# A list of further products of zeros, in other tilings of TensorE's array, behind the first 22: an attention and gMLP block on one core

## The chip, the core and the metric

The kernel runs on one NeuronCore of one Trainium2 chip. The metric is the time of one execution on the device, in microseconds (us). The engines are PE (TensorE, the matrix engine; its weight loads are shown as PEld), DVE (VectorE), ACT (ScalarE), POOL (GpSimd) and SP (SyncE, which issues most DMAs). Each works through its own queue in order, and they wait for each other by semaphores.

## The reference

One token sequence x of 2048 rows and 512 columns is normalised, and the sum of x, an attention block and a gated MLP of the normalised x is returned. All data are float32.

```python
# S, D, H = 2048, 512, 32;  Dh = 16;  F = 1792, Fh = 896
def _A_ref(x, wqkv, wo):
    q, k, v = split(x @ wqkv)                    # 32 heads of 16
    p = softmax(q @ k.T * Dh ** -0.5)
    return (p @ v) @ wo
def _B_ref(x, w_in, w_sp, b_sp, w_out):
    z = gelu(x @ w_in)
    z1, z2 = z[..., :Fh], layernorm(z[..., Fh:])
    g = w_sp @ z2 + b_sp[:, None]                # over the 2048 rows
    return (z1 * g) @ w_out
xn = layernorm(x)
return x + _A_ref(xn, wqkv, wo) + _B_ref(xn, w_in, w_sp, b_sp, w_out)
```

## The kernel before

The instructions of every engine are written out in an order that the program fixes while it is built (a manual schedule). A planner inside it keeps a clock of its own for each engine and decides from these clocks which product comes next; on the chip only the resulting order and the semaphores count.

**Opening.** The four groups of 512 rows of x are loaded (`load_x`), together with the weights of the first query and key columns and of the values. Then come, on PE, `WARM` = 22 products of zeros: `zeror` (128 x 128 zeros, stationary) times `brow` (128 x 512 zeros, streamed) into one bank of the PSUM tile `dps`. They use the type float32r, which PE takes in one pass; plain float32 is taken in two. Behind them a list of words, `STEPS`, is worked off by the class `First`, one method for each letter. The words that matter here, with their rows and columns as digits:

- S, R, N: statistics of two blocks of 128 rows on DVE (`s`), the scale by ACT's square root and DVE's reciprocal (`r`, L1044 to L1046), the normalisation by POOL (`n`, L1055).
- T: four transposes of 128 x 128 on PE into a PSUM tile (`t`, L1060). E: the block is split into a high part by ACT and a rest by DVE (`e`, through `split`, L244).
- Q: twelve products of 128 rows and 512 columns for a query or key block (`q`, through `mm3`, L247 to L249). F: their result is split and stored to scratch memory. L: loaded back as stacks.
- VH, VL, V, VE: weights and products of the values. M, X: the first products for the maxima of the scores (L1132) and their reduction on DVE (L1137).

The four PSUM tiles `dps`, `sl[0]`, `sl[1]`, `sl[2]` (two banks each) are taken in turn by T, Q, V and M, beginning with `sl[0]`. The order of the words begins like this; each engine gets its part in this order:

```python
STEPS = (
    "S00 S01 R00 WH0 N00 WL0 R01 N01 S10 S11 T01 T02 WH1 R10 E01 R11 T00 N11 T03 E02 WL1 N10 E00 VH2* E03 S21 ..."
```

**Steady part.** After the opening, PE works in turns. A turn has score blocks (L1245, two products on row halves that run side by side), blocks for the maxima (L1259, likewise), slots of dense work (L1310: projections, MLP and spatial products, each slot a pair on the two row halves), and then the values (`values`, L1352): 16 products of plain float32, each with 128 rows and 32 columns of the array, four column quarters side by side. Where PE would have nothing to do, a pair of zeros is put in (`filler`, L1324). ACT takes the exponentials, DVE the maxima (L840), POOL splits weights. At the end come the last normalisations and output products, among them products on groups of 32 rows (L984). A matmul's tiling of the array follows from its operands: the partitions on which they start, the number of rows, and the number of columns.

Of the kernel before, what the change touches and what calls it, by code (L numbers as in the profile page):

```python
# [16 lines left out]
P = 128  # L17
# [30 lines left out]
WARM = 22  # L48
# [20 lines left out]
def fused_block(ctx, tc, x, wqkv, wo, w_in, w_spT, b_sp, w_out, out):  # L69
    nc = tc.nc  # L70
# [28 lines left out]
    zeror = cp.tile([P, P], F32R, name="zeror")  # L99
# [3 lines left out]
    brow = cp.tile([P, 512], F32R, name="brow")  # L103
# [29 lines left out]
    dps = ps.tile([P, 2, 512], F32, tag="d", name="dps", bufs=1)  # L133
    sl = [ps.tile([P, 2, 512], F32, tag=f"s{i}", name=f"sl{i}", bufs=1) for i in range(3)]
# [3 lines left out]
    def raw(t):  # L138
        return t.bitcast(F32) if t.dtype == F32R else t
# [999 lines left out]
    def init_rows(a, put):  # L1139
        for j in range(2):  # L1140
            row = 64 * j + KS
            for r in range(2):
                put(kst[a][row + r:row + r + 1, :], cscr[0:1, :])

    engines = {mybir.EngineType.PE, mybir.EngineType.Activation, mybir.EngineType.DVE, mybir.EngineType.Pool, mybir.EngineType.SP}
    with tc.manual_schedule(engines=engines):
# [15 lines left out]
        braw = t512("braw")[0:16, 0:P]  # L1162
        move(braw, b_sp)
        init_rows(0, move)
        for _ in range(WARM):
            nc.tensor.matmul(dps[:, 1, :], zeror, brow, start=True, stop=True)
        first = First(w0r, w0, wvr, wv, braw)
        for word in STEPS.split():
            first.step(word)
# [302 lines left out]
```

## Time and profile before

| | |
|---|---|
| time, median of 2 runs | 1834.91 us (1834.79 and 1835.03) |
| span of the profiled execution, first to last instruction | 1830.4 us (its own time is not listed apart from the two runs) |
| PE busy | 1800.6 us, 98% of the span, 14742 matmul records |
| DVE, ACT, POOL busy | 1443.2, 1211.4, 684.5 us |
| products of zeros at the start | 2.01 to 9.72 us |
| granted TensorE clock, mean | 0.999 |

The profile shows one execution. Each view gives rows with a start and a duration, both in us, the engine, the line of the kernel (L1166 is line 1166), the operation, the tiles (output<-inputs), the shapes and a count. For a matmul, "64*128 64x512" is the part of the array that its weights take (rows times columns) and the streamed operand. Matmuls are pipelined and their ends are modelled, so that a row's duration contains time in which the next matmul runs already; from start to start is the safer measure. A wait ends with what released it, shown behind "<-".

### The profile page before, as it was taken

The page shows a single profiled execution, that of the slowest core. Times are in us where ns is not written, and L with a number is a line of the kernel's source. Part 1 is how long each engine was busy: PE and PEld are TensorE (multiplying, and loading weights), DVE is VectorE, ACT ScalarE, POOL GpSimd, SP SyncE. Part 2 cuts the span into 40 slices and gives each one's busy share as a digit, 9 for nine tenths or more (in the row PEclk, how much of TensorE's full clock was granted, in tenths as well). Part 3 has the DMA queues.
Part 4 walks back from the last instruction along what each step waited for, and adds up shares of the span by engine and source line. Part 5 has one row for each costly group of instructions (what it writes and reads, how often), then busy time and mean ns, then how long its engine had stood idle before and what let it go on. Part 6 is the DMA issues. An engine that isn't in the chain of part 4 may idle for free.

```text
span 1830.4 us, 38100 instructions
## 1 busy us (share of the span) xinstructions
PE 1800.6 (98%) x14742; PEld 1087.6 (59%) x14742; DVE 1443.2 (79%) x1696; ACT 1211.4 (66%) x1329; POOL 684.5 (37%) x786
## 2 busy tenths in 40 slices
PE   9999999999999999999999999999999999999998
PEld 6666566666556565565656655656566665656543
DVE  8857787888888787787877887778778877888882
ACT  4257777888877777666666665666666665666655
POOL 5452241777767776212532244103422140002201
PEclk9999999999999999999999999999999999999999
DMA  7876654433664237647757568655757477466423
GB/s 265 280 240 227 201 190 128 123 114 114 180 190 132 95 105 209 163 137 186 227 144 204 159 188 201 166 143 158 190 146 181 141 210 170 121 156 168 136 88 104
DMA packets 214910, 305.64 MB, mean 167 GB/s; under 512 B 37744, under 2 KB 107952, under 8 KB 214720
## 3 DMA queue, kind: packets, MB, share of 16 engines
q1 hardware_dynamic: 207240, 275.93, 53.3%
q0 software_dynamic: 7488, 27.27, 4.3%
q8 instruction: 116, 1.90, 0.4%
q14 instruction: 66, 0.54, 0.1%
HBM read 193.27 MB, written 109.85 MB: 166 GB/s over the span
## 4 chain that ended last, share of the span: by engine, by line
PE 89%; DVE 5%; DMA 3%; issue 1%; SPq 1%; ACT 1%; POOL 0%; DVEq 0%; ACTq 0%; POOLq 0%
PE dps L1310 35%; PE sl L1352 24%; PE sl L1245 14%; PE sl L1259 12%; DVE mm L840 4%; PE dps L1324 1%; SPq L142 1%; DMA wsp_14r<-in_w_spT 1%; DMA zs<-z2scr 1%; DMA mscr<-ms 0%; PE sl L984 0%; DMA x<-in_x 0%; ACT pf L86 0%; DMA qst<-mscr 0%; DMA qst<-qscr 0%
## 5 line engine op out<-in xcount | busy, mean ns | idle before, releaser
L840 DVE TENSOR_REDUCE mm<-sl 128x2 f32<-128x1024 f32 x1008 | 1208.3, 1222 | 186.0 <-PE sl L1259 177.4
L86 ACT ACTIVATE pf<-sl 128x1024 f32<-128x1024 f32 x1024 | 1043.1, 1026 | 326.7 <-PE sl L1245 288.6
L1352 PE MATMUL sl<-pf,vall 128*32 128x512 f32 x4096 | 467.9, 595 | 0.6 <-DVE on L974 0.6
L1245 PE MATMUL sl<-qst,kst 50*128 50x512 f32 x2048 | 434.6, 417 | 7.7 <-DVE mm L840 2.2
L1259 PE MATMUL sl<-kst,qst 48*128 48x512 f32 x2016 | 414.9, 404 | 3.9 <-DVE mm L840 2.6
L1310 PE MATMUL dps<-wsp,zs 64*128 64x512 f32 x2352 | 381.6, 392 | 0.9 <-DMA zs<-z2scr 0.6
L1245 PEld LDWEIGHTS sl<-qst,kst 50*128 50x128 f32 x2048 | 194.4, 184 | 220.3 <-issue 81.6
L1352 PEld LDWEIGHTS sl<-pf,vall 128*32 128x32 f32 x4096 | 119.2, 109 | 266.5 <-issue 234.9
L1259 PEld LDWEIGHTS sl<-kst,qst 48*128 48x128 f32 x2016 | 191.8, 185 | 104.2 <-ACT pf L86 49.5
L1310 PEld LDWEIGHTS dps<-wsp,zs 64*128 64x128 f32 x2352 | 228.7, 187 | 36.8 <-DMA zs<-z2scr 1.2
L86 ACT ACTIVATE e<-sl 128x512 f32<-128x512 f32 x64 | 38.3, 598 | 189.9 <-PE sl L1352 177.8
L1374 DVE TENSOR_TENSOR e<-sl,e 128x512 f32<-128x512 f32 x64 | 44.2, 691 | 130.2 <-PE sl L1352 80.5
L743 POOL TENSOR_TENSOR hhl<-z1i,hhl 128x512 fp32r<-128x512 f32 x28 | 35.9, 1292 | 280.6 <-ACT hhl L86 280.6
L1310 PE MATMUL dps<-w,xt 64*128 64x448 f32 x768 | 110.5, 368 | 1.7
L1310 PE MATMUL dps<-wout,hp 64*128 64x512 f32 x672 | 110.5, 393 | 0.1
L891 POOL TENSOR_TENSOR ob<-ob 128x512 f32<-128x512 f32 (+1 forms) x16 | 20.6, 1287 | 173.0 <-DMA ob<-rscr 173.0
L1310 PEld LDWEIGHTS dps<-w,xt 64*128 64x128 f32 x768 | 73.7, 186 | 16.1 <-issue 8.4
L1310 PEld LDWEIGHTS dps<-wout,hp 64*128 64x128 f32 x672 | 64.2, 187 | 10.4 <-issue 0.6
L397 POOL TENSOR_TENSOR qkhl<-qr,qkhl 128x512 fp32r<-128x512 f32 x24 | 30.3, 1280 | 97.3 <-ACT qkhl L86 83.0
L887 POOL TENSOR_TENSOR ob<-ob 128x512 f32<-128x512 f32 (+1 forms) x16 | 20.6, 1287 | 99.3 <-DMA ob<-escr 99.3
L1310 PE MATMUL dps<-wf,zs 64*128 64x512 f32 x336 | 55.5, 392 | 0.1
L1310 PE MATMUL dps<-xnT,wqk 64*128 64x512 f32 x288 | 47.9, 394 | 0.3
(298 smaller groups left out, 1692.4 us busy)
## 6 DMA issues: line engine op xcount, KB each, us to landing
zs<-z2scr SPq DMA_DIRECT2D x192, 256.0 KB
escr<-e SPq DMA_DIRECT2D x60, 256.0 KB
hscr<-hhl POOLq DMA_DIRECT2D x28, 512.0 KB, 5.9
qst<-qscr SPq DMA_DIRECT2D x60, 192.0 KB
kst<-kscr SPq DMA_DIRECT2D x60, 192.0 KB
qscr<-qkhl SPq DMA_DIRECT2D x16, 512.0 KB
kscr<-qkhl SPq DMA_DIRECT2D x16, 512.0 KB
xt<-xscr SPq DMA_DIRECT2D x64, 128.0 KB
```

What stands on the lines that cost most here:

```text
L86: return nc.scalar.activation(out, in_, func, **kw)
L142: nc.sync.dma_start(raw(dst), raw(src))
L397: nc.gpsimd.tensor_sub(hl[:, 1, :], raw_, hl[:, 0, :].bitcast(F32))
L743: nc.gpsimd.tensor_sub(hl[:, 1, :], z1, hl[:, 0, :].bitcast(F32))
L840: nc.vector.tensor_reduce(mmax[g][:, :, t, kc], sl[k], AX.X, ALU.max)
L887: nc.gpsimd.tensor_add(both_[rows, 0, :], both_[rows, 0, :], both_[rows, 1, :])
L891: nc.gpsimd.tensor_mul(both_[rows, 0, :], both_[rows, 0, :], both_[rows, 1, :])
L1245: nc.tensor.matmul(sl[k][:, j, :], kst[p % 2][rows, kt * P:(kt + 1) * P], qst[p % 2][rows, c * 512:(c + 1) * 512], start=True, stop=True)
L1259: nc.tensor.matmul(sl[k][:, j, :], qst[p % 2][rows, tt * P:(tt + 1) * P], kst[p % 2][rows, kc * 512:(kc + 1) * 512], start=True, stop=True)
L1310: nc.tensor.matmul(bank_of(bank)[:, :w], lhs, rhs, start=go, stop=stop)
L1352: nc.tensor.matmul(sl[k][cols:cols + VW, 0, :], vpack(kt + r, 2 * p + j), pf[:, j * 512:(j + 1) * 512], start=n % CYC == 0, stop=n % CYC = ...
L1374: nc.vector.tensor_add(e, sl[k][:, 0, :], e)
```

## The change

Behind the 22 products stands a list of 112 more, before the first word of `STEPS`. All of them multiply zeros by zeros; nothing reads the results. `halves_of` issues pairs on the two row halves into the two banks of `dps`, with 512 or 16 streamed columns and 128, 64 or 32 columns of the array; `whole` issues products on all 128 rows, with 128, 64 or 32 columns; `quarters` issues four plain float32 products on the four column quarters into one bank of `sl[0]`; `eighths` issues eight, on the four quarters and two row halves, into both banks of `sl[0]`.

```diff
-        for _ in range(WARM):
-            nc.tensor.matmul(dps[:, 1, :], zeror, brow, start=True, stop=True)
+        def halves_of(n, cols=512, m=P):
+            for _ in range(n):
+                for b, r in enumerate((0, 64)):
+                    nc.tensor.matmul(dps[:m, b, :cols], zeror[r:r + 64, :m], brow[r:r + 64, :cols], start=True, stop=True)
+
+        def whole(n, m=P):
+            for _ in range(n):
+                nc.tensor.matmul(dps[:m, 1, :], zeror[:, :m], brow, start=True, stop=True)
+
+        def quarters(n):
+            for _ in range(n):
+                for u in range(4):
+                    cols = slice(32 * u, 32 * u + 32)
+                    nc.tensor.matmul(sl[0][cols, 0, :], raw(zeror)[:, cols], raw(brow), start=True, stop=True)
+
+        def eighths(n):
+            for _ in range(n):
+                for u in range(4):
+                    cols = slice(32 * u, 32 * u + 32)
+                    for b, r in enumerate((0, 64)):
+                        nc.tensor.matmul(sl[0][cols, b, :], raw(zeror)[r:r + 64, cols], raw(brow)[r:r + 64], start=True, stop=True)
+
+        whole(WARM)
+        for fn, *a in ((halves_of, 3), (quarters, 2), (halves_of, 3), (eighths, 2), (halves_of, 3), (halves_of, 1, 16), (quarters, 2), (halves_of, 1, 16), (halves_of, 3),
+                       (quarters, 2), (whole, 3), (quarters, 2), (whole, 3), (halves_of, 3), (halves_of, 4, 512, 64), (whole, 4, 64), (whole, 4, 32), (halves_of, 4, 512, 32)):
+            fn(*a)
         first = First(w0r, w0, wvr, wv, braw)
         for word in STEPS.split():
             first.step(word)
```

## The prediction

> **What bounds the kernel now.** I read the page's first part and its chain first, then the order of instructions at the start, since the edit stands there.
>
> ```profile
> span 1830.4 us, 38100 instructions
> PE 1800.6 (98%) x14742; PEld 1087.6 (59%) x14742; DVE 1443.2 (79%) x1696; ACT 1211.4 (66%) x1329; POOL 684.5 (37%) x786
> PE 89%; DVE 5%; DMA 3%; issue 1%; SPq 1%; ACT 1%; POOL 0%; DVEq 0%; ACTq 0%; POOLq 0%
> ```
>
> PE is busy for 98% of the span and carries 89% of the chain that ended last. Whatever makes the start of the real work later is therefore unlikely to be made good afterwards: there is 30 us of PE idle in the whole span (1830.4 - 1800.6). Next, the order of instructions at the start. Columns: start, duration, engine, line, operation, tiles, shapes, count, and in brackets the idle time before and what ended it.
>
> ```profile
> 2.01 7.87 PE L1166 MATMUL dps<-brow,zeror 128*128 128x512 f32 x22 [2.01 <-POOL brow L104]
> 9.72 0.27 PE L1060 MATMUL sl<-ident,x 128*128 128x128 f32 x1
> 11.73 1.20 PE L1060 MATMUL sl<-ident,x 128*128 128x128 f32 x9 [0.42 <-POOL x L1055]
> 12.09 0.60 ACT L86 ACTIVATE xnT<-sl 128x512 fp32r<-128x512 f32 x1 [0.51 <-PE sl L1060]
> 13.01 0.68 DVE L244 TENSOR_TENSOR xnT<-sl,xnT 128x512 fp32r<-128x512 f32 x1
> 13.61 0.15 DVE L1045 RECIPROCAL rs<-rs 128x2 f32<-128x2 f32 x1
> 14.06 3.45 POOL L1055 TENSOR_SCALAR x<-x,rs 128x512 f32<-128x512 f32 x4 [2.38 <-DVE rs L1046]
> 17.57 0.98 PE L1060 MATMUL sl<-ident,x 128*128 128x128 f32 x7 [0.23 <-POOL x L1055]
> ```
>
> The 22 products of zeros hold PE from 2.01 to 9.72; then the first transposes of x come, and the fourth of them (11.73) waits for POOL. So about 2 us of what is put between the zeros and the transposes would be hidden by work that PE waits for anyway. Behind that stands a loop through the engines: ACT splits the transposed block (step E01, 12.09), DVE takes the rest (13.01), then DVE finishes the second pair's scale (13.61), then POOL normalises four rows (14.06), then PE transposes them (17.57). ACT and DVE are in order, and the second pair's square root and reciprocal stand behind E01. So if E01 is late, POOL's 14.06 and PE's 17.57 are late by as much.
>
> The opening by stages: busy time of PE, PEld, DVE, ACT, POOL, each with its count, then granted clock and DMA; below it, what PE waits for from 13 to 55 us.
>
> ```profile
> 9.50:13.00 3.50, 2.42 (x17) 1.68 (x16) 3.27 (x10) 1.01 (x3) 2.17 (x3) 1.00 1.04 384
> 13.00:18.00 5.00, 4.22 (x21) 2.80 (x20) 4.90 (x12) 2.34 (x6) 3.94 (x5) 1.00 1.04 381
> 18.00:33.00 15.00, 15.00 (x84) 12.33 (x82) 14.01 (x34) 10.93 (x23) 11.49 (x13) 1.00 0.54 190
> 33.00:55.00 22.00, 22.00 (x106) 15.85 (x105) 18.05 (x20) 5.58 (x10) 2.02 (x3) 1.00 0.72 249
> 55.00:60.00 5.00, 4.23 (x19) 2.71 (x18) 3.35 (x4) 0.60 (x1) 0.00 (x0) 1.00 0.96 374
> 60.00:80.00 20.00, 17.59 (x136) 12.35 (x134) 16.25 (x19) 6.01 (x7) 14.95 (x20) 1.00 0.90 285
> PE sl L247 <- DVE xnT L244: 0.4, 1, 0.4
> PE sl L1060 <- POOL x L1055: 0.2, 1, 0.2
> PE sl L249 <- DVE xnT L244: 0.2, 1, 0.2
> ```
>
> From 13 to 18 DVE is busy for 4.90 of 5; from 18 to 55 PE is busy without a gap; from 13 to 55 PE's waits are 0.8 us in all. So there is no slack behind E01 that a delay could eat: first DVE sets the pace, then PE.
>
> **What the change adds.** Nothing is removed, no wait is added, and no DMA moves. Behind the 22 products stand 112 products of zeros, all on PE and in front of the first transpose. They write dps and sl[0], which PE itself overwrites later, in its own order. I need the price of each tiling.
>
> ```profile
> 14.55 0.39 PE L247 MATMUL sl<-xnT,wqk 128*128 128x512 f32 x1
> 15.47 0.39 PE L248 MATMUL sl<-xnT,wqk 128*128 128x512 f32 x1
> 107.73 1.54 PE L1310 MATMUL sl<-kst,xnT 64*128 64x512 f32 x12
> 109.09 1.54 PE L1310 MATMUL dps<-qst,xnT 64*128 64x512 f32 x12
> 24.94 0.44 PE dps L1060 x4
> 31.80 0.39 PE L249 MATMUL sl<-xnT,wqk 128*128 128x512 f32 x1
> 32.12 0.50 PE L1132 MATMUL sl<-kst,qst 48*128 48x512 f32 x2
> 32.55 0.66 PE L1060 MATMUL sl<-ident,x 128*128 128x128 f32 x4
> 33.04 0.60 PE L1060 MATMUL dps<-ident,x 128*128 128x128 f32 x4
> 87.61 0.41 PE L1310 MATMUL dps<-kst,xnT 64*128 64x512 f32 x2
> 87.95 3.64 PE L1352 MATMUL sl<-pf,vall 128*32 128x512 f32 x32
> 91.52 0.50 PE L1245 MATMUL sl<-qst,kst 50*128 50x512 f32 x2
> 91.86 0.40 PE L1259 MATMUL sl<-kst,qst 48*128 48x512 f32 x2
> 115.02 3.64 PE L1352 MATMUL sl<-pf,vall 128*32 128x512 f32 x32
> 118.59 0.50 PE L1245 MATMUL sl<-qst,kst 50*128 50x512 f32 x2
> 1814.52 1.13 PE L984 MATMUL sl<-sel,on 32*128 32x512 f32 x4
> 1815.58 1.07 PE L1352 MATMUL sl<-pf,vall 128*32 128x512 f32 x8
> ```
>
> The short row at 24.94 is one of the chain's pieces: start, time that it holds on the chain, engine, tile, line, count. Durations of matmuls overlap, so I go by starts.
> - Whole rows, 512 columns: L247 at 14.55 and L248 at 15.47 are four products apart, (15.47 - 14.55) / 4 = 0.23 us each.
> - A row pair: twelve records are six pairs, (109.09 - 107.73) / 6 = 0.227; 0.23 taken. Two halves together cost what one whole product costs.
> - A switch of tiling, there and back: from 31.80 to 33.04 run a whole product (0.23), a pair (0.23) and four transposes (0.44 by the row at 24.94), 0.90 in all. It took 1.24, so 0.34 for two switches, 0.17 each.
> - Column quarters on plain float32: one turn of the attention values is 16 products in the code and 32 records in the trace, so a float32 product is two records. From 87.61 to 91.86 stand two pairs (0.46), two switches (0.34) and four sets of four quarters: (4.25 - 0.80) / 4 = 0.86 a set.
> - Eighths (half the rows, a quarter of the columns, float32): not in the trace. The nearest row is L984, two float32 products on different row groups and banks: 1815.58 - 1814.52 = 1.06, switches included. One after the other they would be two times 0.86, so row groups run side by side. I take a set of eight at 0.86; the other end is 1.72, if the two row halves take turns.
> - Fewer columns of the array (64, 32) on the one-pass type: not in the trace. Nearest are the pair and the whole product, 0.23 a slot. The other end is the float32 pace of two passes, 0.43 a slot, since the only products in 32 columns are of that type. I take 0.23: the stream of 512 elements is the same.
> - Sixteen streamed columns: not in the trace; between nothing and 0.23, nearest the transpose, which streams 128 at 0.11; 0.1 taken.
>
> The sum:
> - halves_of(3) five times: 15 pairs x 0.23 = 3.45
> - quarters(2) four times: 8 sets x 0.86 = 6.9
> - eighths(2): 2 sets x 0.86 = 1.7
> - whole(3) twice: 6 x 0.23 = 1.4
> - fewer columns: 4 pairs + 4 + 4 whole + 4 pairs = 16 slots x 0.23 = 3.7
> - 16 streamed columns: 2 pairs x 0.1 = 0.2
> - switches: between the 18 entries 17 boundaries, of which the two between halves of 512 and of 16 columns that touch change nothing, so 15; with the one into the list and the one out of it 17, x 0.17 = 2.9
>
> That is 20.3 us on PE. The first transpose then starts at 9.72 + 20.3 = 30.0; x is there by then, so its four need 0.33 + 0.27 and end at 30.6. ACT's E01 starts there instead of at 12.09, ends at 31.25, and DVE's part starts at 31.3 instead of 13.01: **18.3 us later**. The two microseconds that went are PE's waits for POOL before 12.09. DVE's next steps and POOL's four rows follow with the same spacing, and from 18 us on PE is gapless, so the 18.3 us is carried to the end of the opening. The stores, loads and weight fetches that SP and POOL issue behind it move with it, because each stands behind a step of the opening in its queue; what ran early, the loads of x and the weights, is over either way.
>
> Can anything later give time back? PE idles 0.8 us at 55 to 60 and 2.4 at 60 to 80, but for engines and DMAs that run behind the same opening and are shifted as well. I take nothing. The span becomes 1830.4 + 18.3 = 1848.7. The profiled execution's own time isn't listed; the two runs of before are 1834.79 and 1835.03, 4.5 us over the span. I keep that: **1853 us**, 1.0% more. A measurement of this kernel can tell about 2% from no change, so this counts as the same.
>
> Two rules of the Trainium skill bear on the sum. For the switch, the row gives 0.17. "TensorEngine Tiling (Array Packing)", Key Properties, says that a change of tiling mode, not merely of the tile, drains TensorE. It gives no price; by it, the changes among 128, 64 and 32 columns count as switches too, as I count them, and the sum stays; if the array treated them as one mode, two changes, 0.3 us, would go. For repeated whole products, the row gives 0.23 from start to start. "TensorE: Matmul & The Clock Gate", Part 3, The mechanism, says that a weight load overlaps running matmuls only where the row group differs. By it, the 14 whole products, which follow each other on all rows, would each pay their load besides; the rows at 14.55 and 15.47 speak against it, since each of those products loads weights of its own on all 128 rows and four of them take 0.92.
>
> **The rivals.**
> - *The unseen forms are dear*: eighths that take turns add 2 x 0.86 = 1.7, few columns at two passes 16 x 0.2 = 3.2, switches as dear as a whole round trip (0.34) 2.9. All three: 18.3 + 7.8 = 26.1, so 1861.
> - *The opening gives more back*: switches that cost nothing among zeros take 2.9 off, and PE's idle time between 13 and 80 us (0.8 + 0.8 + 2.4) is all slack for a late start: 18.3 - 2.9 - 4.0 = 11.4, so 1846. Against it: those gaps are waits on shifted work.
> - *The pace changes, faster*: the list leaves the array in a state in which pairs run at a full pace that they don't have now. The slow pace of the start gives a size for it:
>
> ```profile
> 7.64 2.24 PE L1166 MATMUL dps<-brow,zeror 128*128 128x512 f32 x9
> ```
>
>   The last nine products of zeros start from 7.64 on, 0.23 apart ((9.72 - 7.64) / 9); the thirteen before them took (7.64 - 2.01) / 13 = 0.433. Half of that is 0.217, 0.013 under today's 0.23. PE has 14742 records, of which the values' are 4096 (1024 blocks, two products each, two records a product); the rest is at most 5,300 pairs, 5,300 x 0.013 = 69 us: 1853 - 69 = 1784, 2.8% faster than before. Against it: zeros have run ahead of this kernel's pairs already and pairs hold 0.227; and a turn of the values takes 3.57 the first time (87.95 to 91.52) and the next (115.02 to 118.59), so there is no cost of a first use that could be paid early.
> - *The clock falls back, slower*: products in few columns at the end of the list count as too little work, and the array drops to the 0.43 pace for the opening's 37 gapless microseconds (18 to 55). Each would cost (0.43 - 0.23) / 0.23 = 0.87 more: 32 us, so 1853 + 32 = 1885, 2.7% slower. It decides from 18.4 us of extra delay on, 21 us of slow clock. Against it: the granted clock is 1.00 in 9.5 to 13, where PE ran only 2.42 of 3.5 us, and stays so.
> - *The list isn't on the path*, because PE waits for x anyway: 1835. The waits before 12.09 are 2 us against 20, so this can hardly be.
>
> **How the numbers follow.** The forecast with its sizes within some 4 us (1849 to 1857) 0.74; dear forms (1857 to 1862) 0.10; more given back (1844 to 1849) 0.09; faster pace 0.03; slow clock 0.02; not on the path 0.02. The range for 8 in 10 takes in the ends of the unknown costs: 1846 to 1861. Faster by over 2% is the pace alone, 0.03; slower by over 2% is the clock, 0.02; the rest, 0.95, is within 2%.
>
> **What would show it.** In the profile after, the transposes at L1060's code begin near 30 us; the span is near 1849; PE has 160 records more (112 products, of which the 48 in float32 count twice); the list's stretch by starts is 20 us, with quarters at 0.86 a set; DVE's first xnT starts near 31.3 and POOL's second four rows near 32.4; everything from there stands 18 us later than before, with the same distances, to the end. I am wrong if the shift at 60 us isn't the shift at the end, if the eighths or the narrow products have a pace of their own, or if pairs run at other than 0.227.

## The result and the profile after

The changed kernel took 1850.24 us (median of two runs, 1847.45 and 1853.02) against 1834.91: ratio 1.0083, 95% interval 1.0065 to 1.0102. So it is slower by 0.8%, which is within 2%. The forecast was 1853 in a range of 1846 to 1861. The profiled execution is the one of 1853.02 us.

The first part and the chain of its page:

```profile
span 1851.0 us, 38420 instructions
PE 1821.3 (98%) x14902; PEld 1096.0 (59%) x14902; DVE 1443.6 (78%) x1696; ACT 1212.2 (65%) x1329; POOL 684.5 (37%) x786
PE 89%; DVE 5%; DMA 3%; issue 1%; SPq 1%; ACT 1%; POOL 0%; DVEq 0%; POOLq 0%; ACTq 0%
```

PE has 160 records more (14902 - 14742), as many as foretold, and is busy 20.7 us longer. DVE, ACT and POOL do what they did before. The span grew by 20.6 us.

The order of instructions, from the zeros to the work behind the list (lines are 24 higher than before from the steps on, and the products of the list stand at L1168, L1172, L1178 and L1185):

```profile
2.01 7.45 PE L1172 MATMUL dps<-brow,zeror 128*128 128x512 f32 x22 [2.01 <-POOL brow L104]
9.39 0.96 PE L1168 MATMUL dps<-brow,zeror 64*128 64x512 f32 x6
10.28 1.92 PE L1178 MATMUL sl<-brow,zeror 128*32 128x512 f32 x16
12.14 0.98 PE L1168 MATMUL dps<-brow,zeror 64*128 64x512 f32 x6
13.04 1.95 PE L1185 MATMUL sl<-brow,zeror 64*32 64x512 f32 x32
14.92 0.97 PE L1168 MATMUL dps<-brow,zeror 64*128 64x512 f32 x8
15.83 1.92 PE L1178 MATMUL sl<-brow,zeror 128*32 128x512 f32 x16
17.68 1.08 PE L1168 MATMUL dps<-brow,zeror 64*128 64x16 f32 x8
18.70 1.92 PE L1178 MATMUL sl<-brow,zeror 128*32 128x512 f32 x16
...
24.21 1.88 PE L1168 MATMUL dps<-brow,zeror 64*128 64x512 f32 x14
26.02 2.07 PE L1172 MATMUL dps<-brow,zeror 128*64 128x512 f32 x8
28.02 1.11 PE L1168 MATMUL dps<-brow,zeror 64*32 64x512 f32 x8
29.06 1.53 PE L1060 MATMUL sl<-ident,x 128*128 128x128 f32 x12
...
29.76 0.60 ACT L86 ACTIVATE xnT<-sl 128x512 fp32r<-128x512 f32 x1 [18.32 <-PE sl L1060]
30.39 0.69 DVE L244 TENSOR_TENSOR xnT<-sl,xnT 128x512 fp32r<-128x512 f32 x1 [17.45 <-ACT xnT L86]
31.44 3.45 POOL L1055 TENSOR_SCALAR x<-x,rs 128x512 f32<-128x512 f32 x4 [19.71 <-DVE rs L1046]
34.95 0.98 PE L1060 MATMUL sl<-ident,x 128*128 128x128 f32 x7 [0.24 <-POOL x L1055]
```

The list runs from 9.39 to 29.06. Read the brackets at its end: ACT had been idle for 18.32 us, DVE for 17.45, POOL for 19.71, and each was released by the engine before it in the loop that begins with the first transposes. DVE, POOL and PE's next transposes stand 17.4 us later than before (30.39 against 13.01, 31.44 against 14.06, 34.95 against 17.57).

The first turn of the attention values, and the stages of the opening between:

```profile
36.00:51.00 15.00, 14.92 (x79) 11.86 (x78) 14.03 (x33) 10.54 (x22) 10.91 (x12) 1.00 0.54 188
51.00:73.00 22.00, 22.00 (x106) 15.80 (x105) 18.03 (x20) 5.49 (x10) 2.00 (x2) 1.00 0.78 270
104.55 3.64 PE L1376 MATMUL sl<-pf,vall 128*32 128x512 f32 x32
39.20 0.42 PEld L1060 LDWEIGHTS sl<-ident,x 128*128 128x128 f32 x4 [0.32 <-DVE xnT L244]
```

From 51 to 73 PE is without a gap again, with the 106 products that it had from 33 to 55. From 36 to 51 it lacks 0.08 us and five products: four transposes wait with their weight loads for DVE (the last line), and the shift grows there from 17.4 to 17.9. The first turn starts at 104.55 against 87.95: 16.6 us late. Where the 1.3 us between went is told under "Nothing given back". From there to the end this execution loses 4 us more, and most of that is in one place, at a spatial unit. First the waits of PE there, then the instructions, then the windows of 7 us of this execution and, below it, of another execution of the same kernel (`repeat`, of 1847.2 us span):

```profile
PE dps L1334 <- DMA zs<-z2scr: 1.6, 2, 0.9
1148.79 0.50 PE L1334 MATMUL dps<-wsp,zs 64*128 64x512 f32 x1 [0.74 <-DMA zs<-z2scr]
1150.14 1.22 PE L1334 MATMUL dps<-wsp,zs 64*128 64x512 f32 x3 [0.86 <-DMA zs<-z2scr]
1150.74 1.05 PE L1269 MATMUL sl<-qst,kst 50*128 50x512 f32 x2
1151.17 1.05 PE L1283 MATMUL sl<-kst,qst 48*128 48x512 f32 x2
1155.37 1.49 PE L1376 MATMUL sl<-pf,vall 128*32 128x512 f32 x12
1148.00:1155.00 7.00, 5.40 (x31) 4.15 (x30) 2.99 (x3) 2.47 (x3) 1.26 (x1) 0.76 0.54 150
```

```profile
1153.01 1.92 PE L1376 MATMUL sl<-pf,vall 128*32 128x512 f32 x16
1148.00:1155.00 7.00, 6.20 (x50) 3.72 (x54) 5.18 (x10) 2.37 (x3) 0.63 (x1) 1.00 0.50 143
```

PE waits twice for a load of zs, and then the granted clock is 0.76 in the mean of the window: pairs stand 0.43 apart (1150.74 to 1151.17) instead of 0.23. The values behind begin at 1155.37; in the other execution, where the clock stayed at 1.00, they begin at 1153.01. Of these 2.4 us, 0.8 were there before the slow pace (the product at 1150.14 starts at 1149.30 in the other execution), most of it longer waits for zs; the other 1.5 are the clock. Both differ from one execution to the next.

### The profile page after: what moved, and what is told of

The parts are those of the page before. It is cut to its first block, busy times and chain, and to the rows that moved or that the text cites. A ratio compares the mean times of both kernels' runs of the same rounds, so it can differ in the third digit from the quotient of the medians.

```text
span 1851.0 us, 38420 instructions
## 1 busy us (share of the span) xinstructions
PE 1821.3 (98%) x14902; PEld 1096.0 (59%) x14902; DVE 1443.6 (78%) x1696; ACT 1212.2 (65%) x1329; POOL 684.5 (37%) x786
## 4 chain that ended last, share of the span: by engine, by line
PE 89%; DVE 5%; DMA 3%; issue 1%; SPq 1%; ACT 1%; POOL 0%; DVEq 0%; POOLq 0%; ACTq 0%
PE dps L1334 35%; PE sl L1376 23%; PE sl L1269 14%; PE sl L1283 12%; DVE mm L840 4%; DMA zs<-z2scr 1%; PE dps L1348 1%; PE dps L1172 1%; SPq L142 1%; DMA qst<-mscr 1%; PE sl L247 1%; PE sl L248 0%; PE sl L249 0%; DMA mscr<-ms 0%; PE sl L1178 0%
## 5 line engine op out<-in xcount | busy, mean ns | idle before, releaser
L891 POOL TENSOR_TENSOR ob<-ob 128x512 f32<-128x512 f32 (+1 forms) x16 | 20.6, 1285 | 174.2 <-DMA ob<-rscr 174.2
```

Source lines behind the costliest of these rows:

```text
L891: nc.gpsimd.tensor_mul(both_[rows, 0, :], both_[rows, 0, :], both_[rows, 1, :])
```

## The experiments

My theory (A): the list costs its own length on PE, less the 2 us in which PE would have waited for x; what the tilings are counts only through their durations. Against it stood that the tilings leave something behind (B), that the opening has slack (C), that the cost comes from holding up the other engines (D), and that the clock takes such products for less work (E). Each kernel is the changed one with the edit shown, unless said otherwise.

**repeat**, unedited.

> The changed kernel once more, as it is. In its first profile everything stood 17.4 us late when DVE's first xnT began (30.39 against 13.01), 16.6 at 57 us, and 20.6 at the end: 2.4 of that came in one place, near 1150 us, where pairs on wsp and zs waited for a DMA and then ran at 0.43 apart. Theory A (the list delays the first transposes by its own length, less 2 us; what is added later is chance of DMA waits): first xnT at 30.0 to 30.8, 16.5 to 17.5 late at 80 us, and at the end anything from 15 to 21 late, with or without the wait near 1150; time 1847 to 1853. Theory B (the list leaves something behind that costs later): the 2.4 us near 1150 come again at the same place, and the end is 20 or more late.

```profile
30.86 0.69 DVE L244 TENSOR_TENSOR xnT<-sl,xnT 128x512 fp32r<-128x512 f32 x1 [17.98 <-ACT xnT L86]
105.06 3.64 PE L1376 MATMUL sl<-pf,vall 128*32 128x512 f32 x32
```

Measured: 1849.22 us against 1834.23 for the kernel before beside it, ratio 1.0081 (1.0069 to 1.0093). The first values are 17.1 late (105.06 - 87.95), the end of the span 16.8 (1847.2 - 1830.4), and the clock is at 1.00 near 1150, as shown above. The first xnT came 0.06 outside the expected 30.0 to 30.8, because the first 22 products ended 0.49 later than in the first profile. The late loss didn't come again: that speaks for A against B.

**plain_86**, the same length in one tiling.

```diff
-        for fn, *a in ((halves_of, 3), (quarters, 2), ...):
-            fn(*a)
+        whole(86)
```

> The list is replaced by 86 whole products of zeros behind the 22, all of one tiling: 86 x 0.23 = 19.8 us, as long as the list took (9.30 to 29.06). Theory A (only the length counts): first xnT at 30.4 as with the list, time as with the list within 2 us. Theory B (the tilings count beyond their time, by a state of the array or its clock): the opening as with the list, but pairs behind it at another pace than with the list, or 3 us less at the end in every run.

```profile
29.77 0.69 DVE L244 TENSOR_TENSOR xnT<-sl,xnT 128x512 fp32r<-128x512 f32 x1 [16.69 <-ACT xnT L86]
103.42 3.64 PE L1374 MATMUL sl<-pf,vall 128*32 128x512 f32 x32
```

Measured: 1848.86 us, ratio 1.0079 (1.0067 to 1.0091), the same as the list beside it. First xnT at 29.77, 0.6 before the expected 30.4, and from there to the first values 73.65 us, against 74.16 with the list (104.55 - 30.39). The 0.5 between is the wait of the transposes at 38.53, which stands in `repeat` too but neither here nor in first_nine or list_alone, which issue other tilings as well; in both executions that have it, one short DVE instruction ahead of it (L1046) lasted 1.3 us instead of 0.16, and why isn't shown. So the tilings leave nothing behind that costs or gains: B falls, and so does the rival of a faster pace. The first profile says the same of the pace: the values that start at 541.69 before start at 558.50 with the list, 16.8 late after 16.6 at the first values, so 450 us of pairs ran as before.

**first_nine**, the list's first nine entries alone.

```diff
-        ... (halves_of, 3),
-                       (quarters, 2), (whole, 3), ... (halves_of, 4, 512, 32)):
+        ... (halves_of, 3)):
```

> Only the first nine entries of the list. They took 9.4 us in the profile (9.30 to 18.70), so the first transposes start 10.3 us earlier than with the whole list. Theory A: first xnT at 20.1, the opening 7.1 late against before, time 1840 to 1844, some 7 over before. A rival that the opening has slack which a short list finds first (C): under 4 us over before. Theory B, a state that the later entries (few columns, whole rows between quarters) leave: not 7 but under 5 or over 10.

```profile
20.61 0.69 DVE L244 TENSOR_TENSOR xnT<-sl,xnT 128x512 fp32r<-128x512 f32 x1 [7.70 <-ACT xnT L86]
94.25 3.64 PE L1375 MATMUL sl<-pf,vall 128*32 128x512 f32 x32
```

Measured: 1838.52 us against 1834.23, ratio 1.0023 (1.0009 to 1.0037). The first values stand 6.3 us late (94.25 - 87.95). By the order of instructions A's 7 holds within 1 us; by time it is 4.3 (1.7 to 6.8 by the interval), under the 1840 to 1844 that I expected and in the band that I had given to B. The time alone doesn't decide. The profile speaks for A: first xnT is 7.6 late and the first values 6.3, 73.64 us apart as in plain_86 (73.65); the 1.3 between is a wait for a load in the profile of the kernel before, told under "Nothing given back". So nothing was lost or won by what the later entries are. The profiled execution is the slowest of the seven (1841.93), with a fall of the clock at 1141.

**plain_8**, eight whole products in the list's place (`whole(8)`), as long as the cover.

> Eight whole products in the list's place, 1.84 us. Theory A: PE waits for POOL's normalised rows before the fourth transpose anyway, some 2 us, so the first xnT starts at 13.0 to 13.2 and the time is that of before within 1 us. A rival by which every product ahead of the transposes counts: 1.8 us more than before, first xnT at 14.8.

```profile
2.01 9.43 PE L1172 MATMUL dps<-brow,zeror 128*128 128x512 f32 x30 [2.01 <-POOL brow L104]
11.28 1.63 PE L1060 MATMUL sl<-ident,x 128*128 128x128 f32 x12
12.77 0.68 DVE L244 TENSOR_TENSOR xnT<-sl,xnT 128x512 fp32r<-128x512 f32 x1
```

Measured: 1834.07 us, ratio 0.9997 (0.9987 to 1.0007). The transposes start 1.56 us later than before (11.28 against 9.72), now twelve in one piece without a wait for POOL, and DVE's first xnT isn't late at all (12.77 against 13.01). So 1.56 us of delay are covered.

**early_norm**, statistics, scales and normalisations of all four groups ahead of the first transposes.

```diff
-    "S00 S01 R00 WH0 N00 WL0 R01 N01 S10 S11 T01 T02 WH1 R10 E01 R11 T00 N11 T03 ...
+    "S00 S01 R00 WH0 N00 WL0 R01 N01 S10 S11 WH1 R10 R11 N11 N10 S21 R21 S20 R20 N21 N20* S31 R31 S30 R30 N31 N30* "
+    "T01 T02 E01 T00 T03 E02 WL1 E00 VH2* E03 VH3* ...
```

> The changed kernel, with the statistics, scales and normalisations of all four groups of x (the words S, R, N) moved ahead of the first transposes, into the time in which the list runs and DVE idles (17.4 us in the profile). DVE loses 8 statistics of 0.66 and their aggregates, some 6.7 us, from the stretch behind the list, and POOL 9 us. Theory A (behind the list PE itself is the bound: without a gap from 36 to 73 us): the first xnT as with the list, 30.4; the opening ends at most 1 us earlier; time 1847 to 1852. Rival C (DVE sets the pace of the opening, so that work moved under the list gives back much of it): the first products of the steady part 4 us or more earlier than with the list, time 1843 to 1846.

The first xnT, the first values, and the stage behind (lines one higher):

```profile
29.73 1.29 DVE L245 TENSOR_TENSOR xnT<-sl,xnT 128x512 fp32r<-128x512 f32 x2 [4.42 <-ACT xnT L87]
103.19 3.64 PE L1377 MATMUL sl<-pf,vall 128*32 128x512 f32 x32
36.00:51.00 15.00, 15.00 (x84) 12.31 (x84) 9.53 (x15) 9.07 (x17) 6.77 (x7) 1.00 0.67 237
```

Measured: 1849.33 us, ratio 1.0075 (1.0060 to 1.0091). DVE's busy time from 36 to 51 fell from 14.03 to 9.53, and the time from first xnT to first values from 74.16 to 73.46. The first xnT came at 29.73, 0.7 before the expected 30.4, because the first 22 products ended earlier. So 4.5 us taken off an engine that looked like a bound gave 0.7, and 0.5 of it is the wait for DVE at 38.53, which plain_86 is without as well: PE was the bound behind the list. C falls.

**list_late**, the list behind the whole opening.

```diff
         for word in STEPS.split():
             first.step(word)
+        for fn, *a in ((halves_of, 3), (quarters, 2), ...):
+            fn(*a)
```

> The list stands behind the whole opening instead of in front of the first transposes. Theory A (it costs its length where PE has work, less the waits of PE that it fills): the opening is that of before; the list takes 19.8 us again, filling at most some 2 us of PE's waits; time 1834 + 17 to 20, so 1850 to 1854. Rival D (the cost in front came from holding up ACT, DVE and POOL through the first transposes, and PE alone would hide part of it behind the opening): under 12 us more than before.

```profile
13.02 0.69 DVE L244 TENSOR_TENSOR xnT<-sl,xnT 128x512 fp32r<-128x512 f32 x1
61.26 0.97 PE L1168 MATMUL dps<-brow,zeror 64*128 64x512 f32 x6 [1.32 <-DVE mm L1137]
80.83 0.86 PE L1283 MATMUL sl<-kst,qst 48*128 48x512 f32 x6
106.83 3.64 PE L1376 MATMUL sl<-pf,vall 128*32 128x512 f32 x32
```

Measured: 1852.57 us, ratio 1.0095 (1.0079 to 1.0112). The list takes 19.57 us (61.26 to 80.83); it even adds a wait, since it writes `dps` while DVE still reduces it (1.32). The first values are 18.9 us late, 2.3 more than with the list in front. So the place matters by about the 2 us of cover: D falls.

**list_alone**, the list without the 22 products ahead of it.

> The list without the 22 whole products ahead of it, starting at 2.01 at the slow pace. Theory A (the clock rises by any of these tilings as it does by whole products, at 6.7 to 8 us): the list takes 19.8 us and some 2.5 us for the slow start; the first transposes at 24 to 25 us, 4 to 5 us earlier than with the 22; time 1843 to 1848. Rival E (pairs and quarters count as less work for the clock): the slow pace lasts beyond 10 us, and each further microsecond of it adds half a microsecond.

```profile
2.01 1.65 PE L1168 MATMUL dps<-brow,zeror 64*128 64x512 f32 x6 [2.01 <-POOL brow L104]
3.59 3.11 PE L1178 MATMUL sl<-brow,zeror 128*32 128x512 f32 x16
6.63 0.96 PE L1168 MATMUL dps<-brow,zeror 64*128 64x512 f32 x6
24.80 0.69 DVE L244 TENSOR_TENSOR xnT<-sl,xnT 128x512 fp32r<-128x512 f32 x1 [11.95 <-ACT xnT L86]
```

Measured: 1844.34 us, ratio 1.0048 (1.0031 to 1.0065). The first pairs and quarters are slow (1.58 us to the next row instead of 0.89, and 3.04 instead of 1.86), and from 6.63 on the rows have their fast length. The slow pace lasts 4.0 us from the first product (2.01 to 6.04), against 3.2 to 6.0 us in the profiles that begin with whole products: pairs and quarters end it as whole products do, and E falls. The granted clock in the windows doesn't show this, since it reads 1.00 from the start: the trace's first clock entry, which says 1.00, comes only at 6.04 here (7.50 in the kernel before, 6.69 in the changed one), and the pace changes at these times. What I expected of the transposes missed: they start at 23.48, not at 24 to 25, since the slow pace ended sooner than the 6.7 to 8 us.

**no_zeros**, the kernel before without its 22 products.

> The kernel before without any products of zeros. Theory A (what stands ahead of the transposes is only worth its effect on the clock): the first transposes wait for x until 9 us as before, but the array runs at the slow pace (0.43 for a whole product) until it has been busy for some 5 us, so the opening loses 1 to 4 us; time 1835 to 1838. Rival: without the zeros nothing is lost, since PE waits for DVE there: 1834 within 1 us.

```profile
15.22 0.63 PE L248 MATMUL sl<-xnT,wqk 128*128 128x512 f32 x1
15.65 0.63 PE L249 MATMUL sl<-xnT,wqk 128*128 128x512 f32 x1
88.42 3.64 PE L1350 MATMUL sl<-pf,vall 128*32 128x512 f32 x32
```

Measured: 1834.25 us against 1834.41, ratio 0.9991 (0.9981 to 1.0001). The opening does start at the slow pace (0.43 from 15.22 to 15.65; the trace's first clock entry stands at 16.23), but the first values are only 0.5 us late, and the time shows nothing. I expected 1 to 4 us; the rival was right.

## Why the prediction was right

**The list's length.** 20.3 us were worked out; from 9.39 to 29.06 it took 19.7, or 19.8 with 0.1 for the part of the switch into it that falls on the last of the 22. Term by term:
- Quarters, two sets and a switch: 2 x 0.86 + 0.17 = 1.89 foretold, 1.86 measured (10.28 to 12.14), and 1.85 (15.83 to 17.68). A float32 product is two records; in the trace the four first records start together at 10.28 to 10.30, the four second ones at 10.74, and the next set at 11.17. So each record holds its columns for some 0.43, and a float32 product takes nearly four times as long as a float32r one (0.23), not twice; sets of four side by side make up for it.
- Eighths: 1.89 foretold, 1.88 measured (13.04 to 14.92). Row groups and column quarters run side by side, eight records starting within 0.05 us of each other; the other end, 1.72 a set, is out.
- Three pairs and a switch: 0.86 foretold, 0.89 and 0.90 measured (9.39 to 10.28, 12.14 to 13.04).
- The pairs of 16 columns: 0.1 each foretold. The one ahead of quarters cost 0.01 (14.92 to 15.83 is 0.91, against 0.90 without it), the one behind them 0.12 (17.68 to 18.70 is 1.02).
- Few columns: 3.7 and five switches with the three pairs ahead, 0.69 + 3.7 + 0.85 = 5.24 foretold; from 24.21 to 29.06 it took 4.85. This is the term of the list that was too large. The seven pairs from 24.21 took 1.81, one switch more than 7 x 0.23, and the eight whole products from 26.02 took 2.00, likewise: going from 128 to 64 columns, or from 64 to 32, cost nothing where the rows stayed. "TensorEngine Tiling (Array Packing)" of the Trainium skill, Key Properties, says that a change of tiling mode drains TensorE; changes of the rows do cost something here (0.16 to 0.2 each), but at these two no cost shows.

**Weight loads of whole products.** Eight in few columns follow each other from 26.02 to 28.02 at 0.23 and a switch, and in plain_86 the 81 in 128 columns from 9.69 to the transposes at 28.50 take 0.232 each. The rule of "TensorE: Matmul & The Clock Gate" of the Trainium skill, Part 3, The mechanism, that loads overlap running matmuls only where the row group differs, would have made them dearer; the measurement decides against it here. The same section also lets a load into a background weight buffer be pulled ahead, and that agrees.

**The cover and the loop.** 2.0 us of cover were foretold. The transposes start 19.3 later (29.06 against 9.72) and the first xnT 17.4, so the cover is 2.0; plain_8 shows 1.56 of it by itself. That the transposes aren't later by the whole list is an execution's chance: the 22 products ahead of it reached the fast pace sooner here and ended at 9.39 instead of 9.72; in `repeat` they ended at 9.88.

**Nothing given back.** Foretold: nothing. The shift still isn't constant: it is 17.4 at the first xnT, 17.9 from the transposes at 38.53 on, and 16.6 at the first values. The fall of 1.3 stands in one place. Before, PE waited there twice for a load of kst; the first two lines are the kernel before, the last two list_late, whose opening starts as early as that of the kernel before:

```profile
55.92 0.47 PE L1132 MATMUL dps<-kst,qst 48*128 48x512 f32 x1 [0.30 <-DMA kst<-kscr]
57.76 0.50 PE L247 MATMUL sl<-kst,xnT 128*128 128x512 f32 x1
55.59 0.52 PE L1132 MATMUL dps<-kst,qst 48*128 48x512 f32 x2
56.49 0.50 PE L247 MATMUL sl<-kst,xnT 128*128 128x512 f32 x1
```

From the product ahead of the wait (at 55.23) to the one behind it, it made 2.53 us, against 1.22 in list_late (55.27 to 56.49) and with the list (73.16 to 74.38). With the list the wait is gone, but it is gone in list_late and plain_8 too, where nothing is late at this point, and no_zeros has it (0.6 us). So it differs between executions of an opening that isn't shifted, and no run shows that the list took it away. The other waits of PE in front of the first values came again, each as long and as late as the rest: 1.4 us for DVE at L426, 0.6 at L1137, and 0.6 before against 0.7 for ACT. That these gaps are only shifted, as the prediction had it, holds.

**The total.** The step that was off is the way from the span to the time. The prediction worked out a span of 1848.7 and added 4.5 us, the distance of two runs' times from the span of the profiled execution of the kernel before (1830.4), whose own time isn't on record. Wherever a run has both on record, the time is 1.7 to 3.3 us over the span, here 2.0 (1853.02 - 1851.0 and 1847.45 - 1845.4); so that execution was probably neither of the two runs. With 2.0 the same working gives 1850.7, against 1850.24 measured. That it comes so close is partly luck: the two runs lie 5.6 us apart, and the five of `repeat` have a median of 1849.22.

As a difference, 18.3 us were foretold, and 15.3 measured first, 15.0 in `repeat` (12.7 to 17.1 by its interval). The profiled execution of the kernel before, from which the 18.3 start, was a quick one: its span is 1830.4, and the 19 beside `repeat` have a median of 1831.8. Of the rest, 0.5 is the list; what else there is lies within what runs of the kernel before differ by (1831.62 to 1840.51 us, the slowest with the lowest granted clock, 0.997).

One sign of being wrong that the prediction named does show in the first profile: the shift near 60 us (17.9 before the wait for kst, 16.6 behind it) isn't the shift at the end (20.6). In `repeat` 17.1 at the first values became 16.8 at the end, so what came later in the first profile is that execution's and not the list's. The two rivals beyond 2% didn't come: the pace is the same behind the list, and in the opening the clock stayed at 1.00.

## What to carry to other kernels

In this kernel, products that nobody reads cost their full length as soon as they were longer than the wait they filled. Measure that wait first by what the next engine in the loop starts on (here DVE's first xnT, 2 us), then price the rest from start to start. A shift at the beginning of a program whose bound engine has no gaps arrived at the end, whatever the other engines could do meanwhile: 4.5 us less DVE work gave 0.7. To know whether a loss or a gain belongs to an edit, follow the shift of the same instruction along two traces, and look for the same change in a run without the edit: here 2.4 us near 1150 weren't in the repeated run, and a wait of 1.3 us that seemed to be saved is missing in list_late too. And take a span and a time from the same execution.

## What the runs showed of the hardware that I had not expected

- PE's clock halved twice right behind waits far shorter than the slow stretch that followed: after two waits of 0.74 and 0.86 us near 1150 the granted clock was 0.50 from 1150.15 to 1153.57, and in first_nine for as long at the same unit, from 1141.2 on. It doesn't follow from the waits alone: in early_norm 1.2 us and in list_alone 1.5 us of waits for the same tile left the clock at 1.00. What decides stays open.
- The 22 products of zeros that the kernel had before brought nothing that can be measured (no_zeros, 0.9991): the slow pace at the start delays the opening by about 1 us (15.22 against 14.08 for the same product at L248), and half of that is gone by the first values.
- Narrowing the columns of the array from 128 to 64 and to 32 cost no switch where the rows stayed (1.81 us for seven pairs, 2.00 for eight whole products); changing the rows cost 0.16 to 0.2 us.
